# An adaLN attention and GLU block: eight query blocks of 256 instead of four of 512, with side work between the scores

## The chip, the cores and the metric

The kernel runs on one core of one Trainium2 chip. The metric is device time in microseconds. The core has five engines that run at the same time: TensorE (PE; its weight loads are listed apart as PEld), VectorE (DVE), ScalarE (ACT), GpSimd (POOL) and SyncE (SP), which here only issues transfers. Each engine works through its own instructions in the order in which the program was written; between engines only semaphores make one wait for another.

## The reference

The computation is a transformer block on 2048 tokens of width 512: a conditioned layer norm, multi-query attention with 32 heads of width 16 that share one key and one value, and a gated product of two projections.

```python
mod = (_silu(c) @ w_mod).reshape(1, 6, 1, -1)          # six rows of 512
h = _layernorm(x) * (1 + ca) + sa
q = (h @ wq) split into 32 heads of 16;  k = h @ wk;  v = h @ wv
scores = einsum("bhqd,bkd->bhqk", q, k) * 16 ** -0.5
o = softmax(scores) @ v
x = x + ga * (o @ wo)
h = _layernorm(x) * (1 + cb) + sb
x = x + gb * (((h @ w_gate) * (h @ w_up)) @ w_down)    # inner width 1792
```

Inputs and output are 32-bit floats. The kernel scales the large operands and splits each into two 16-bit halves, so that a product becomes three 16-bit products that are added up.

## The kernel before, in words

**Units and steps.** The 2048 queries are taken in four blocks (`NB`) of 512 (`BT`). A unit is four heads of a block, so a block has eight units (`UB`) and there are 32 (`NU`). A unit has 32 steps. In each step TensorE writes two tiles of scores with queries on partitions (`max_mm`, written to banks named mx), whose row maxima VectorE takes (L565); two tiles of scores with keys on partitions, the maxima already subtracted (`qk_exp`, banks sc), whose exponentials ScalarE takes (L601, tile P); and one product of earlier exponentials with the values (`pv`, 32-bit, L609). Maxima run 38 steps (`LEAD`) ahead of the exponentials: the first 38 steps have maxima alone and share their time with the first norm and the projections of keys, values and the first queries. Once a unit's maxima are complete they are transposed and split (`max_rows`, L577 to L583) and sent by two transfers into the stationary tile sst (L586), as two more rows of the score product.

**Row halves.** All these products use 64 of the array's 128 rows and 32 of its columns at a time: four matmuls (`quarters`, L474) make one row half of a tile. Work on the upper and the lower row half can be in the array at the same time, if they write to different banks.

**Side work.** Everything else on TensorE in the loop goes through a list (`fill`): the query projections (`q_proj`, tiles h and wq), the output projection (`wo_work`, och and wo), the gate and up products (h2T with wg and wu) and the down product (glu with wd). A `duo` takes two output tiles at once, one on each row half, and swaps them half way; a pair is one matmul group on each row half, eight matmuls. At the end of each step `fill_gap` writes a burst of up to three pairs, at a rate that `pace` works out from the due times of all that is listed. The work that belongs to a block begins one unit after the block's last.

**Rows after attention.** `pv_out` adds two partial sums on VectorE (L621), sends heads to a tile oc and the softmax sums to memory (L628, L629); `normalise` fetches them (L636), inverts (L639), spreads them (L641, L643), multiplies and splits on POOL (L648 to L651). `wo_work` ends with the second norm's statistics (L697 to L715), and four single items transpose the normed rows (L740) into h2T (L747 to L750). Those four items run alone: no pair is written until they are through.

**Late weights.** Three weight matrices and wo are read twice in slices into tiles wsl (L870). The first time POOL squares them and adds them up (L877, L879), ones on TensorE sum over partitions (L889) and VectorE takes the maxima of these sums (L892); that gives scales. The second time POOL scales and splits them (L966 to L974). `side_step` writes one such item every 2.5 steps.

**The tail.** After the last unit the last block's rows still need their output projection, norm, gate, up and down products. They run as plain matmuls on all 128 rows and columns (`plain`, L521). What is left in `fill` by then (`RESERVE`) covers the waits of the last normalisation and norm.

Of the kernel before, what the change touches and what calls it, by code (L numbers as in the profile page):

```python
# [13 lines left out]
F32 = mybir.dt.float32  # L14
# [7 lines left out]
NB = 4  # L22
BT = S // NB
UB = H // 4
NU = NB * UB
# [3 lines left out]
ABS_GAP = 2.5  # L29
SPLIT_GAP = 2.5  # L30
NSC = 2
NMX = 2
NP = 5
CW = 32
# [5 lines left out]
RESERVE = 31000.0  # L40
TR_GAP = 8
# [4 lines left out]
Q_BURSTS = {16: 4, 17: 2, 18: 2, 19: 2, 20: 2, 22: 6, 23: 6}  # L46
DUE = 12
QDUE = 236
# [5 lines left out]
def adaln_mqa_glu_kernel(ctx: ExitStack, tc: tile.TileContext, x_in, wq_in, wk_in, wv_in, wo_in,  # L54
# [48 lines left out]
    wqs = work.tile([128, KC, 64], F32, name="wqs", tag="xl", bufs=3)  # L103
    nc.scalar.dma_start(wqs, wq_in[:, 0:64].rearrange("(k p) n -> p k n", p=128))
# [8 lines left out]
    wk3 = work.tile([128, KC, 2, 64], F32, name="wk3", tag="och", bufs=4)  # L113
    nc.gpsimd.memset(wk3, 0.0)
    wq0 = [work.tile([128, KC, 2, 64], F32, name="wq0", tag="och", bufs=4) for _ in range(2)]
    for w in wq0:
        nc.gpsimd.memset(w, 0.0)
    wqst = [work.tile([128, D], F32, name="wqst", tag=("gf", "oc")[k // 2], bufs=2) for k in range(KC)]
# [83 lines left out]
    h16 = big.tile([128, 2, KC, S], F16, name="h16", tag="big")  # L202
# [85 lines left out]
    for h in range(4):  # L288
        nc.gpsimd.tensor_copy(wq0[h // 2][:, :, h % 2, 0:48].rearrange("p k (r e) -> p k r e", e=16),
                              wqs[:, :, None, 16 * h:16 * h + 16].to_broadcast([128, KC, 3, 16]))  # L290
# [4 lines left out]
    mrow = work.tile([128, 256], F32, name="modrow", tag="xl", bufs=3)  # L295
# [39 lines left out]
    def q0_mm(p, ks=range(KC)):  # L335
        if 0 in ks:
            pqs[p] = ps_misc() if p else ps_pv()
        for k in ks:
            nc.tensor.matmul(pqs[p], wq0[p][:, k].rearrange("p a r -> p (a r)"), hf(0, k),
                             start=(k == 0), stop=(k == KC - 1))  # L340
# [62 lines left out]
    def h_halves(b, ks=range(KC)):  # L403
        cs = slice(b * BT, (b + 1) * BT)
        for k in ks:
            in_halves(h16[:, 0, k, cs], h16[:, 1, k, cs], hf(b, k),
                      None if b else fwd[:, 0:1], nc.scalar if b > 1 else nc.gpsimd)
# [18 lines left out]
    first = {0: lambda: q0_mm(1, KA), 1: lambda: (q0_mm(1, KB), ln_stats(6)),  # L426
# [15 lines left out]
    def v_mm(k):  # L442
# [3 lines left out]
        for i, (wl, hl) in enumerate(TERMS):  # L446
            for b in range(NB):
                nc.tensor.matmul(p[32 * b:32 * b + 32, :], wv[:, wl, k, :], h16[:, hl, k, b * BT:(b + 1) * BT],
# [18 lines left out]
    class Group:  # L467


        def __init__(self, n, op, pre, post, mid=True):  # L470
            self.n, self.op, self.pre, self.post, self.mid = n, op, pre, post, mid

    def quarters(p, left, right, start=True, stop=True):
        return [nc.tensor.matmul(p[c:c + CW, :], left[:, c:c + CW], right, start=start, stop=stop)  # L474
                for c in range(0, 128, CW)]

    def half(p, g, i, r, start, stop):
        left, right = g.op(i)
        return quarters(p, left[64 * r:64 * r + 64], right[64 * r:64 * r + 64], start, stop)
# [4 lines left out]
    def duo(g0, g1, tags=("misc", "spare")):  # L484

        ps = g0.pre(tag=tags[0]), g1.pre(tag=tags[1])
        n = g0.n
        mark = None
        for turn in range(2):
            for i in range(n):  # L490
                for r in range(2):
                    ms = half(ps[r ^ turn], (g0, g1)[r ^ turn], i, r, turn == 0 and i == 0,
                              turn == 1 and i == n - 1)
                    if mark is not None:
                        tc.add_manual_dep(ms[0].ins, mark.ins.name, SYNC, reason="row halves of one bank in turn")
                        mark = None
                if turn == 0 and i == n - 1 and cur["mark"]:
# [779 lines left out]
```

## Time and profile before

| | |
|---|---|
| median of 3 runs | 1772.2 us (1771.98 to 1772.65) |
| the profiled execution | 1771.55 us, span 1769.7 us |
| granted TensorE clock | 0.994 of full speed |
| busy share PE / DVE / ACT / POOL | 96 / 81 / 74 / 32% |
| maxima on VectorE (L565) | 2048 of 685 ns |
| exponentials on ScalarE (L601) | 2048 of 601 ns |
| plain matmuls (L521) | 720, 379 ns each with the pipeline's own delay |

Rows of the profile's groups read: line, engine, operation, tile written, tiles read, shape, count, then the busy time of the group in us and the mean of one in ns, then the idle time of the engine before them and what ended it. Matmuls overlap, so a sum of their means is far more than the busy time. Windows give, for each stretch, its length and the busy time and count of each engine in it, then the clock, the share of the DMA engines and GB/s.

### The profile page before, as it was taken

The page shows a single profiled execution, that of the slowest core. Times are in us where ns is not written, and L with a number is a line of the kernel's source. Part 1 is how long each engine was busy: PE and PEld are TensorE (multiplying, and loading weights), DVE is VectorE, ACT ScalarE, POOL GpSimd, SP SyncE. Part 2 cuts the span into 40 slices and gives each one's busy share as a digit, 9 for nine tenths or more (in the row PEclk, how much of TensorE's full clock was granted, in tenths as well). Part 3 has the DMA queues.
Part 4 walks back from the last instruction along what each step waited for, and adds up shares of the span by engine and source line. Part 5 has one row for each costly group of instructions (what it writes and reads, how often), then busy time and mean ns, then how long its engine had stood idle before and what let it go on. Part 6 is the DMA issues. An engine that isn't in the chain of part 4 may idle for free. (4 is left out here: it accounts for less than half of the span.)

```text
span 1769.7 us, 86400 instructions
## 1 busy us (share of the span) xinstructions
PE 1707.4 (96%) x39203; PEld 878.6 (50%) x39203; DVE 1442.1 (81%) x2353; ACT 1301.8 (74%) x2319; POOL 562.5 (32%) x788
## 2 busy tenths in 40 slices
PE   6899999999999999999999999999999999999999
PEld 3334444433345565565545555565545555543444
DVE  7899999999998888899998888899999998922210
ACT  3478888878878878887788888887888888893110
POOL 5714444436657852210032222110032121221130
PEclk9999999999999999999999999999999999999999
DMA  5212222212222210000100000000100000001000
GB/s 195 100 32 80 60 80 62 77 46 73 80 74 58 66 34 15 11 19 23 42 23 18 11 10 20 7 16 24 48 16 18 12 18 11 14 7 41 19 0 24
DMA packets 49115, 70.04 MB, mean 40 GB/s; under 512 B 15270, under 2 KB 29418, under 8 KB 48748
## 3 DMA queue, kind: packets, MB, share of 16 engines
q1 hardware_dynamic: 47164, 64.33, 12.2%
q8 instruction: 306, 5.01, 1.2%
q14 instruction: 61, 0.50, 0.1%
q10 hardware_dynamic: 1584, 0.20, 0.1%
HBM read 51.12 MB, written 8.92 MB: 34 GB/s over the span
## 5 line engine op out<-in xcount | busy, mean ns | idle before, releaser
L565 DVE TENSOR_REDUCE mpart<-mx 128x1 f32<-128x512 f32 x2048 | 1329.0, 685 | 125.9 <-PE mx L474 36.1
L601 ACT ACTIVATE P<-sc 128x512 f32<-128x512 f32 x2048 | 1177.0, 601 | 259.9 <-PE sc L474 203.7
L609 PE MATMUL pv<-P,vst 64*32 64x512 f32 x8192 | 1080.8, 598 | 0.0
L474 PE MATMUL mx<-kst,sst 48*32 48x512 f16 x8192 | 808.4, 383 | 35.7 <-DVE mpart L565 27.2
L474 PE MATMUL sc<-sst,kst 50*32 50x512 f16 x8192 | 818.5, 379 | 5.3 <-ACT P L601 4.5
L474 PEld LDWEIGHTS <-sst 48*32 48x32 f16 x8192 | 335.6, 90 | 514.4 <-issue 420.9
L474 PEld LDWEIGHTS <-kst 50*32 50x32 f16 x8192 | 264.2, 92 | 92.7 <-issue 60.7
L474 PE MATMUL misc<-h2T,wu 64*32 64x512 f16 x4032 | 294.8, 376 | 0.0
L474 PE MATMUL misc<-h2T,wg 64*32 64x512 f16 x4032 | 294.2, 376 | 0.0
L609 PEld LDWEIGHTS pv<-P,vst 64*32 64x32 f32 x8192 | 197.8, 105 | 17.9 <-ACT P L601 0.8
L791 POOL TENSOR_TENSOR gf<-gf,g 128x512 f32<-128x512 f32 x42 | 53.7, 1279 | 344.2 <-ACT gf L790 344.2
L474 PEld LDWEIGHTS <-wu 64*32 64x32 f16 x4032 | 111.0, 92 | 36.1
L474 PEld LDWEIGHTS <-wg 64*32 64x32 f16 x4032 | 112.9, 92 | 30.7 <-issue 1.5
L474 PE MATMUL misc<-wd,glu 64*32 64x512 f16 x2688 | 112.9, 376 | 0.0
L474 PE MATMUL misc<-h,wq 64*32 64x512 f16 x1536 | 95.4, 377 | 1.2 <-ACT qf L531 1.2
L498 POOL MEMSET token<- 1x1 f32 x43 | 3.8, 88 | 281.4 <-PE misc L474 216.7
L783 ACT ACTIVATE g<-misc 128x512 f32<-128x512 f32 x56 | 33.4, 596 | 77.0 <-PE misc L521 75.5
L521 PE MATMUL misc<-wd,glu 128*128 128x512 f16 x336 | 73.2, 379 | 0.0
L474 PEld LDWEIGHTS <-glu 64*32 64x32 f16 x2688 | 60.3, 92 | 23.4 <-issue 0.4
L795 POOL TENSOR_TENSOR glu<-gf,glu 128x512 f16<-128x512 f32 x56 | 65.0, 1161 | 4.7
L793 DVE TENSOR_TENSOR gf<-misc,g 128x512 f32<-128x512 f32 x14 | 9.7, 692 | 62.9 <-PE misc L521 62.9
L621 DVE SCALAR_TENSOR_TENSOR ev<-pv,evs,ev 128x512 f32<-128x512 f32 x32 | 23.7, 742 | 44.5 <-ACT ev L616 44.5
(232 smaller groups left out, 1063.1 us busy)
## 6 DMA issues: line engine op xcount, KB each, us to landing
wsl<-in_B_w_gate_dram SPq DMA_DIRECT2D x32, 224.0 KB
wsl<-in_B_w_up_dram SPq DMA_DIRECT2D x32, 224.0 KB
wsl<-in_B_w_down_dram SPq DMA_DIRECT2D x28, 256.0 KB
sst<-qd SPq DMA_DIRECT2D x186, 32.0 KB
qd<-q SPq DMA_DIRECT2D x16, 256.0 KB
oc<-ev SPq DMA_DIRECT2D x128, 32.0 KB
rr<-ri SPq DMA_DIRECT2D x16, 256.0 KB
xl<-in_A_x_dram SPq DMA_DIRECT2D x16, 256.0 KB
```

Source lines behind the costliest of these rows:

```text
L474: return [nc.tensor.matmul(p[c:c + CW, :], left[:, c:c + CW], right, start=start, stop=stop) for c in range(0, 128, CW)]
L498: mark = nc.gpsimd.memset(token, 0.0)
L521: nc.tensor.matmul(p, left, right, start=i == 0, stop=i == g.n - 1)
L565: nc.vector.tensor_reduce(mparts[u][:, a, p, t, kc:kc + 1], m, axis=AX.X, op=OP.max)
L601: nc.scalar.activation(ptl[u, kt, a][:, p, :], t, AF.Exp)
L609: nc.tensor.matmul(pvb[u, r][32 * j:32 * j + 32, :], vst[ks, kt, :], ptl[u, kt, a][ks, p, :], start=(kt == 0), stop=(kt == KT - 1))
L621: nc.vector.scalar_tensor_tensor(ev, pvb[u, 1], evs, ev, op0=OP.mult, op1=OP.add)
L783: nc.scalar.activation(st["g", f], p, AF.Copy, scale=2.0 ** -45)
L791: nc.gpsimd.tensor_tensor(gf, gf, st["g", f], op=OP.mult)
L793: nc.vector.tensor_tensor(gf, p, st["g", f], op=OP.mult)
L795: nc.gpsimd.tensor_tensor(st["glu"][:, 1, f, :], gf, st["glu"][:, 0, f, :], op=OP.subtract)
```

## The change

- The queries are taken in eight blocks (`NQ`) of 256 (`QT`). A unit is now eight heads of such a block, two of them side by side in the 512 columns of a tile, so there are still 32 units of 32 steps with the same score, maximum, exponential and value instructions; a block has four units. `load_q` needs twelve transfers for it instead of six, `pv_out` nine instead of five, and each unit is normalised alone, on half as many columns.
- Gate and up products have 256 tokens and so 256 columns. A group holds two such products side by side in one bank (`parts=2`): sixteen matmuls of half the length to a pair. Down and output products keep their 512 columns and have two tiles of rows to a block.
- A pair may be cut: in a step with side work, its first row half is written between the first exponential's scores with the value product and the second maximum, the other row half after the second scores, and the rest of the burst behind it (`pair_half`).
- The transposes of the second norm leave `fill` and go, two to a block, into the banks of the maxima, at fixed steps after the output projection. The down product of a block waits until after the next block's output projection.
- Row maxima are issued one step later than they are ready, from ScalarE's queue.
- ScalarE squares the late weights, and for wo and the down weights a sum over all takes the place of column sums; items come every 1.5 steps in the first pass and every 2.0 in the second. Products start when the slices they need have been written (`ready`).
- The input of the query projection lies in two tiles, the projections are due at step 140 instead of 236, twice as many run in the first 38 steps, and `RESERVE` falls from 31000 to 20000.

```diff
-UB = H // 4
-NU = NB * UB
+NQ = 8
+QT = S // NQ
+UB = H // 8
+NU = NQ * UB
...
-RESERVE = 31000.0
+RESERVE = 20000.0
...
+    def product(p, g, i, j, rows, start, stop):
+        left, right = g.op(i) if g.parts == 1 else g.op(i, j)
+        w = 512 // g.parts
+        start, stop = start and j == 0, stop and j == g.parts - 1
+        p, left, right = p[:, j * w:(j + 1) * w], left[rows], right[rows]
+        if rows.stop - rows.start == 64:
+            return quarters(p, left, right, start, stop, skip_group_check=g.parts > 1)
+        nc.tensor.matmul(p, left, right, start=start, stop=stop, skip_group_check=g.parts > 1)
...
-            for hl in range(2):
-                nc.sync.dma_start(s[48 + hl:113 + hl:64, :, :], mt[hl])
+
+            def send():
+                for hl in range(2):
+                    nc.scalar.dma_start(s[48 + hl:113 + hl:64, :, :], mt[hl])
+
+            after(1, send)
...
+            if m > 1:
+                nc.scalar.activation(t, t, AF.Square, accum_out=fro[:, m - 2, i:i + 1])
+                return
             acc = ssq[:, c]
-            nc.gpsimd.tensor_tensor(acc if i == 0 else t, t, t, op=OP.mult)
+            nc.scalar.activation(acc if i == 0 else t, t, AF.Square)
...
+    def pair_half(step, r):
+        what = cur["gen"].emit(r)
+        if cur["gen"].done:
+            return
+        credit[0] -= 1.0
+        cur["left"] -= 1
+        cur["turn"] -= 1
...
+            n = 0
+            if fill or cur["gen"]:
+                credit[0] = min(credit[0] + pace(step) / 2, 6.0)
+                n = plan(step)
             max_half(a, 0, 2)
             qk_exp(u, kt, 0, a)
...
             drain_mids()
+            if n:
+                pair_half(step, a)
             max_half(a, 1, 2)
             qk_exp(u, kt, 1, a)
+            if n:
+                pair_half(step, 1 - a)
+                burst(step, n - 1)
             if p == 1:
                 late_max()
-            if fill or cur["gen"]:
-                credit[0] = min(credit[0] + pace(step) / 2, 6.0)
-                if credit[0] >= 1.0:
-                    fill_gap(step)
...
-        gu = [(Group(3 * KC, op(f, 0), pre(f), gate(f)), Group(3 * KC, op(f, 1), ps_misc, up(f))) for f in range(FT)]
-        return gu, [Group(3 * FT, dn(t), ps_misc, fin(t)) for t in range(4)]
+        gu = [(Group(3 * KC, op(f, 0), pre(f), gate(f), parts=2), Group(3 * KC, op(f, 1), ps_misc, up(f), parts=2))
+              for f in range(FT // 2)]
+        return gu, [Group(3 * FT, dn(t), ps_misc, fin(t)) for t in range(2)]
```

How the instructions move, at three places. TensorE in a step amid the gate and up products: mx are the maxima's scores, sc the exponentials', pv the value product, wg and wu the two tiles of a pair. Before, a burst stands behind the second sc; one matmul of each group is shown.

```order
L474 MATMUL mx<-kst,sst_122 32x512
...
L474 MATMUL sc<-sst_120,kst 32x512
...
L609 MATMUL pv<-P,vst 32x512 x4
...
L474 MATMUL mx<-kst,sst_122 32x512
...
L474 MATMUL sc<-sst_120,kst 32x512
...
L474 MATMUL misc<-h2T,wg 32x512
...
L474 MATMUL misc<-h2T,wu 32x512
```

The same in the change:

```order
L485 MATMUL mx<-kst,sst_124 32x512
...
L485 MATMUL sc<-sst_123,kst 32x512
...
L641 MATMUL pv<-P,vst 32x512 x4
...
L485 MATMUL misc<-h2T,wg 32x256
...
L485 MATMUL mx<-kst,sst_124 32x512
...
L485 MATMUL sc<-sst_123,kst 32x512
...
L485 MATMUL misc<-h2T,wu 32x256
```

One row half of a pair has moved between the two maxima, and its four matmuls of 512 columns have become eight of 256.

ScalarE in the first unit: P are exponentials, mt the split row maxima, wsl a slice of weights, fro its sum of squares. Before:

```order
L601 ACTIVATE P<-sc 128x512 x56
L582 ACTIVATE mt_2250<-mxt 16x128
L601 ACTIVATE P<-sc 128x512 x12
L616 ACTIVATE ev<-pv,evs 128x512
L601 ACTIVATE P<-sc 128x512 x32
```

In the change:

```order
L633 ACTIVATE P<-sc 128x512 x4
L923 ACTIVATE wsl,fro<-wsl 128x512
L633 ACTIVATE P<-sc 128x512 x4
L926 ACTIVATE kwb<-wsl 128x448
...
L926 ACTIVATE wsl<-wsl 128x448
L616 DMA sst_124<-mt_2436 2x8x128
L616 DMA sst_124<-mt_2437 2x8x128
```

A square now stands behind every fourth exponential, and the two transfers of the row maxima, which were SP's, stand among the exponentials.

TensorE in the tail, at the first gate and up products of the last block: before and in the change.

```order
L521 LDWEIGHTS wg
L521 MATMUL misc<-h2T,wg 128x512
...
L521 LDWEIGHTS wu
L521 MATMUL misc<-h2T,wu 128x512
```

```order
L495 LDWEIGHTS wg
L495 MATMUL misc<-h2T,wg 128x256
...
L495 LDWEIGHTS wu
L495 MATMUL misc<-h2T,wu 128x256
```

The last block is half as long: 336 matmuls of 512 columns for its gate and up products have become 336 of 256, and it has two tiles of rows for each of the other products instead of four.

More of the change, by code (lines that the diff above doesn't have):

```diff
@@ L481, in adaln_mqa_glu_kernel @@
     token = consts.tile([1, 1], F32, name="token")
     SYNC = mybir.DependencyInfo(mybir.DependencyClass.Sync, mybir.DependencyReason.DATA)
[L484 to L497, printed above, removed]
-                    mark = nc.gpsimd.memset(token, 0.0)
-                    tc.add_manual_dep(mark.ins, ms[-1].ins.name, SYNC, reason="end of a row half")
-                if turn == 0 or i < n - 1:
-                    yield i == n - 1
-        g0.post(ps[0])
-        def late():
-            g1.post(ps[1])
-            after(3, free)
-        def free():
-            spare["held"] -= 1
-        spare["held"] += 1
-        if g1.mid:
-            mids.append(late)
-        else:
-            after(2, late)
@@ new lines, in adaln_mqa_glu_kernel, with __init__, emit, late @@
+    class Duo:
+        def __init__(self, two, tags, marked):
+            self.g = two
+            self.ps = [g.pre(tag=tag) for g, tag in zip(two, tags)]
+            self.n, self.turn, self.i, self.done, self.marked, self.mark = two[0].n, 0, 0, set(), marked, None
+        def emit(self, r):
+            w = r ^ self.turn
+            g, n = self.g[w], self.n
+            for j in range(g.parts):
+                ms = product(self.ps[w], g, self.i, j, slice(64 * r, 64 * r + 64),
+                             self.turn == 0 and self.i == 0, self.turn == 1 and self.i == n - 1)
+                if self.mark is not None:
+                    tc.add_manual_dep(ms[0].ins, self.mark.ins.name, SYNC, reason="row halves of one bank in turn")
+                    self.mark = None
+            self.done.add(r)
+            if len(self.done) < 2:
+                return None
+            self.done.clear()
+            self.i += 1
+            if self.i < n:
+                return None
+            if self.turn == 0:
+                self.turn, self.i = 1, 0
+                if self.marked:
+                    self.mark = nc.gpsimd.memset(token, 0.0)
+                    tc.add_manual_dep(self.mark.ins, ms[-1].ins.name, SYNC, reason="end of a row half")
+                return "swap"
+            self.g[0].post(self.ps[0])
+            spare["held"] += 1
+            if self.g[1].mid:
+                mids.append(self.late)
+            else:
+                after(2, self.late)
+            return "end"
+        def late(self):
+            self.g[1].post(self.ps[1])
+            after(3, self.free)
+        def free(self):
+            spare["held"] -= 1
@@ L519, in plain @@
         for i in range(g.n):
-            left, right = g.op(i)
-            nc.tensor.matmul(p, left, right, start=i == 0, stop=i == g.n - 1)
+            for j in range(g.parts):
+                product(p, g, i, j, slice(0, 128), i == 0, i == g.n - 1)
             if i < g.n - 1:
@@ L846, in m1 @@
         def m1():
-            st["row"] = work.tile([128, D], F32, name="modrow", tag="xl", bufs=3)
+            st["row"] = work.tile([128, D], F32, name="modrow", tag="xl", bufs=NXL)
             nc.scalar.activation(st["row"], st["p"], AF.Copy)
@@ L926, in bc @@
             nc.tensor.matmul(st["p"][:, 0:6], ones6, st["r"][:, 1:7], start=True, stop=True)
+            nc.tensor.matmul(st["p"][:, 8:10], ones, cmx[:, 2:4], start=True, stop=True)
         def scales():
@@ L1066, in open_gate @@
         gate = fill[0][0]
+        if len(gate) > 2 and ready[0] < gate[2]:
+            return False
+        if len(gate) > 3 and step < ln_end.get(gate[3], END) + LN_WAIT:
+            return False
         if gate[0] is None:
@@ L1222, in adaln_mqa_glu_kernel @@
         assert cur["second"] and NU * NSTEP - cur["swapped"] > 2
-        for _ in cur["gen"]:
+        while cur["gen"] is not None:
             drain_posts()
+            burst(NU * NSTEP, 1)
+        drain_posts()
         drain_mids()
```

337 lines of the change are left out of this document (179 added, 158 removed).

## The prediction

> **What bounds the kernel now.** I read the engines' busy shares on the page first, then windows cut at the loop's units, then the waits, the chain that ended last and single stretches of the timeline. All times are in the profiled execution: span 1769.7 us, its own time 1771.55 us, so 1.85 us lie around the span; the median of the runs, 1772.2 us, is 0.04% above it.
>
> The windows below begin and end with a unit's first and last exponential. Columns: stretch and length, then busy us and count for PE, PEld, DVE, ACT, POOL.
>
> ```profile
> PE 1707.4 (96%) x39203; PEld 878.6 (50%) x39203; DVE 1442.1 (81%) x2353; ACT 1301.8 (74%) x2319; POOL 562.5 (32%) x788
> ...
> 93.70:273.40 179.70, 174.44 (x3796) 73.39 (x3796) 168.54 (x278) 153.43 (x269) 69.66 (x71) 0.98 0.21 60
> 229.90:273.40 43.50, 42.54 (x969) 18.38 (x961) 41.42 (x68) 38.71 (x68) 22.05 (x24) 1.00 0.29 81
> 503.00:553.70 50.70, 47.96 (x1137) 25.61 (x1128) 45.70 (x75) 41.85 (x76) 37.84 (x68) 0.97 0.26 70
> 652.20:701.50 49.30, 48.90 (x1409) 30.14 (x1401) 43.37 (x69) 39.70 (x73) 13.86 (x17) 1.00 0.07 17
> 1567.50:1605.80 38.30, 36.46 (x739) 13.29 (x727) 0.75 (x1) 36.30 (x69) 6.20 (x7) 1.00 0.03 7
> 93.70:1605.80 1512.10, 1476.04 (x37717) 777.30 (x37720) 1339.25 (x2151) 1249.61 (x2232) 470.95 (x614) 1.00 0.13 35
> 1605.80:1769.70 163.90, 158.62 (x750) 72.17 (x746) 29.22 (x47) 15.30 (x23) 32.52 (x60) 1.00 0.07 22
> ```
>
> The loop of 32 units is 1512.1 us; behind it stands a tail of 163.9 us in which only TensorE works (158.62 busy). The same windows for the tiles called misc give the side work of a unit; eight matmuls are one pair of row halves:
>
> ```profile
> 229.90:273.40 43.50, 13.19 (x192) 0.00 (x0) 0.00 (x0) 1.39 (x2) 1.00 0.29 81
> 503.00:553.70 50.70, 16.95 (x352) 1.68 (x16) 1.49 (x2) 3.79 (x5) 0.97 0.26 70
> 652.20:701.50 49.30, 25.82 (x624) 0.00 (x0) 0.00 (x0) 3.61 (x6) 1.00 0.07 17
> 1380.60:1428.10 47.50, 22.57 (x488) 0.00 (x0) 0.00 (x0) 3.60 (x6) 1.00 0.05 11
> 1428.10:1474.60 46.50, 22.66 (x480) 0.00 (x0) 0.00 (x0) 2.42 (x4) 1.00 0.07 18
> 1522.20:1567.50 45.30, 22.86 (x484) 0.00 (x0) 0.00 (x0) 2.42 (x4) 1.00 0.05 14
> 1567.50:1605.80 38.30, 10.13 (x216) 0.00 (x0) 0.00 (x0) 2.42 (x4) 1.00 0.03 7
> 93.70:1605.80 1512.10, 613.90 (x13296) 5.05 (x48) 14.83 (x20) 70.24 (x110) 1.00 0.13 35
> ```
>
> A unit with 24 pairs takes 43.5 us, with 60.5 (mean of two) 47.0, with 78 it is 49.3. So a pair costs (47.0 − 43.5)/36.5 = 0.096 us up to 60 and 2.3/17.5 = 0.13 beyond: less than its own time on the array (0.216, below), since the array also waits. In the full units neither VectorE (43.37 of 49.3) nor ScalarE is full; the three engines wait on each other in turn. The whole loop holds (13296 − 48 transposes)/8 = 1656 pairs.
>
> **The tail** is the surest term.
>
> ```profile
> 1641.05 124.77 PE misc L521 x578
> ```
> ```profile
> 1605.80:1769.70 163.90, 156.09 (x720) 70.28 (x720) 1.00 0.07 22
> ```
>
> One plain matmul of 512 columns comes every 124.77/578 = 0.216 us, and 720 of them fill the tail. In the change's order the tail keeps 192 of 512 columns (168 down, 24 output projection) and 384 of 256. A short one costs between half (0.108) and, if the weight load behind it sets the pace, all of 0.216; I take 0.109, by the half, since the row above shows 70.28/720 = 0.098 us of weight load for each, just less. New: 192 × 0.216 + 384 × 0.109 = 83.4; old: 155.5. With 1 us more of idle time, as the cover work is thinner, the tail falls by 71 us (bounds 30 and 72).
>
> **The loop gets what the tail loses.** By the order it now holds 1968 pairs: none in the first unit, then 42.5, 41.5, 43.5, 37 and 31, about 55 in each of the next three, 69.2 in each of the next twenty, then 81, 84 and 59.5. By the two slopes: 37 and 31 pairs, 44.7 + 44.2 = 89; three at 46.5 = 139.4; twenty at 47.0 + 8.7 × 0.13 = 48.1 = 962; 81 pairs 49.7; the next to last 45.3 + 23 × 0.13 = 48.3; the last, where ScalarE is 95% busy and hides pairs, 39.5. The first four are ScalarE's: it now squares the 50 weight slices that POOL squared.
>
> ```profile
> L601 ACT ACTIVATE P<-sc 128x512 f32<-128x512 f32 x2048 | 1177.0, 601 | 259.9 <-PE sc L474 203.7 <-ACT P L601 1.3
> L377 ACT ACTIVATE wqj<-wqst 128x512 f32<-128x512 f32 x4 | 2.5, 628 | 0.1
> L377 ACT ACTIVATION_READ_ACCUMULATOR wqj<-wqst 128x1 f32 x4 | 0.7, 186 | 0.0
> L531 ACT ACTIVATE qf<-misc,qvs 128x512 f32<-128x512 f32 x16 | 11.1, 691 | 4.3 <-PE mx L474 2.3 <-POOL q L533 2.0
> ...
> 1567.50:1605.80 38.30, 34.30 (x64) 1.00 0.03 7
> ```
>
> Where ScalarE alone sets the pace, 64 exponentials are 34.3 us. Four units: 137.2; 32 squares of 448 columns at 0.628 × 448/512 = 0.55, 17.6; 18 with a sum at 0.81, 14.7; 10 projections at 0.69 and some 3 us of small ones, 9.9; in all 179.4, and at the 95% that the last unit reaches 189 us. Before, 179.7. Sum of the loop: 189 + 89 + 139.4 + 962 + 49.7 + 48.3 + 39.5 = 1517.
>
> Added to it: the second norm. The unit at 503 us, which holds it, takes 50.7 with (352 − 16)/8 = 42 pairs, 5.5 above the slope, for four tiles of rows; seven blocks of two tiles, 2.75 each, 19 us (from 0, if that excess was the pause in the side work alone, to 38). And POOL, which splits the weights faster than before:
>
> ```profile
> L972 POOL TENSOR_SCALAR wsl<-wsl,sca 128x448 f32<-128x448 f32 x32 | 20.4, 639 | 22.6 <-DMA wsl<-in_B_w_gate_dram 12.4 <-DMA wsl<-in_B_w_up_dram 10.1
> L973 POOL TENSOR_SCALAR wu<-wsl 128x448 f16<-128x448 f32 x16 | 9.0, 565 | 1.3
> L974 POOL TENSOR_TENSOR wu<-wsl,wu 128x448 f16<-128x448 f32 x16 | 16.6, 1040 | 1.3
> ```
>
> 2.24 us a slice, 17 slices in the sixth unit are 38 us of a unit of 44, beside the halves of the norm and of the first gate, so POOL falls behind there. Late POOL keeps load buffers, SP's later transfers stand behind those loads, and the row sums that VectorE inverts come late. I take 5 us (0 to 10). The loop is then 1541, 29 above before. That 312 more pairs cost so little has a reason: laid over the units of before the two slopes give 1478 of the 1512, and the other 34 are extras that shrink or move (16 the norms, most of the rest the weights' column sums of the first eight units, which the change cuts from 16 to 4).
>
> **Side halves between the scores.** One half now stands between the two row maxima of a step. Does TensorE use it?
>
> ```profile
> 1011.95 0.40 PE L474 MATMUL misc<-h2T,wg 64*32 64x512 f16 x4
> 1012.00 0.60 PE L609 MATMUL pv<-P,vst 64*32 64x512 f32 x4
> 1012.16 0.40 PE L474 MATMUL mx<-kst,sst 48*32 48x512 f16 x4
> 1012.38 0.40 PE L474 MATMUL sc<-sst,kst 50*32 50x512 f16 x4
> ```
>
> In the program mx and sc stand ahead of pv, yet pv, on the other row half, starts first: each half runs on by itself, so a half placed earlier can fill idle time. The most it can bring is a full unit at the pace of the lightest, 48.1 − 43.5 = 4.6 us in each of 20 units, 92 us; the least is nothing. Of some 4.3 halves a step one is moved between the maxima, so I take a quarter, 23 us. The Trainium skill (TensorE: Matmul & The Clock Gate, Part 3, "What overlaps and what doesn't") says that matmuls keep program order in start and end. By that rule the moved half gains nothing and the time would be 23 us more; the pv at 1012.00 ahead of the mx at 1012.16 disagrees.
>
> **The rest.** The head takes 24 more projection pairs, 24 × 0.216 = 5.2 us, bounds 0 and 10. Row maxima from ScalarE's queue:
>
> ```profile
> SPq L586 <- ACT mt L582: 472.1, 27, 38.0
> ...
> PE mx L474 <- DVE mpart L565: 27.2, 73, 1.2
> ...
> PE sc L474 <- ACT P L601: 4.5, 14, 1.1
> ...
> 903.07 0.55 SPq L629 DMA_DIRECT2D rs<-ev  x1
> ```
>
> SP spends 472 us on waiting to send them, but TensorE's scores wait for no transfer, so the move wins nothing. Two issues of 0.55 us a unit now stand among the exponentials: 1.1 us, hidden while ScalarE has 9 us a unit to spare; without that cover 4.4 us in the first four units, inside the 189. SP's own issues (21 small transfers a unit for queries and outputs instead of 11) are 21 × 0.55 = 12 us of 48, on an engine with nothing else to do.
>
> **The sum:** 1769.7 − 71 + 5.2 + 29 − 23 = 1709.9 span, and 1.85 around it: **1712 us**, 3.4% faster.
>
> **Rivals.**
>
> *The short matmuls cannot be fed.* A gate/up pair was 16 instructions on TensorE and is now 32; by the order 1152 of the loop's pairs are such. The densest ten microseconds of a full unit:
>
> ```profile
> 713.80:723.80 10.00, 10.00 (x324) 6.63 (x324) 8.65 (x13) 7.85 (x14) 2.65 (x4) 1.00 0.02 5
> ```
>
> That is 30.9 ns a matmul. A unit with 69 gate/up pairs has 768 + 69 × 16 = 1872 matmuls, 25.7 ns each at 48.1 us; at 30.9 it takes 57.8. Of four units two are dense (+9.7 and +6.8), one mixed (+2), one with down products alone unharmed: 18.6 × 5 = 93, with the early and last units 125 us: 1837, slower. It decides from about 29 ns a matmul. For it: nothing here shows a denser stretch. Against it: the array itself set that pace (10.00 busy), and a burst goes faster:
>
> ```profile
> 60.57 1.06 PE L474 MATMUL misc<-h,wq 64*32 64x512 f16 x32
> 60.57 0.56 PEld L474 LDWEIGHTS <-wq 64*32 64x32 f16 x32 [0.17 <-issue]
> ...
> L474 PE MATMUL misc<-h2T,wg 64*32 64x512 f16 x4032 | 294.2, 376 | 0.0
> ```
>
> 32 weight loads began within 0.5 us. The same page ("Wait — 56ns, not 53.3ns?") puts a floor of about 25 ns between starts, however short the matmul; by it 16 would take 0.40 us, and 1152 such pairs 207 us more if nothing hid it. Four starts of a group lie within 0.40 − 0.376 us in the rows above, so it does not hold across column strips.
>
> *The halves do more.* All of the 92 us: 1643. For it: full units leave 12% of VectorE idle. Against: three quarters of the side work stay in bursts.
>
> *The halves do nothing:* 1735. VectorE's two banks could still set the pace.
>
> *The loop takes all back.* At a full 0.216 for each of 312 added pairs, 67 us instead of the 30 by the slopes, and no help from the halves, the loop is 1541 + 37 = 1578 and the time 1769.7 − 71 + 5.2 + 66 + 1.85 = 1772: no change. For it: TensorE is busy 48.90 of 49.3 in a full unit. Against it: the slopes are measured, and half of that.
>
> **How the numbers follow.** Two measurements can be told apart from about 0.2%, 3.5 us. Forecast 0.48, 1680 to 1730; halves do more 0.16 (1640 to 1680); halves do nothing 0.18 (1730 to 1760). Together 0.82 faster. Not fed 0.10; all taken back 0.08, of which 0.05 within 0.2% of before and 0.03 above: same 0.05, slower 0.13. The range for 8 in 10, 1645 to 1772, leaves out the slow cases and the lower end of the halves.
>
> **What would show it.** Right: a tail of about 92 us with 576 plain matmuls, units of 47 to 48 us at 69 pairs, the first four at 47 each with ScalarE over 90% busy. Wrong: gate/up units longer than down units at equal pairs (feeding); full units of 44 us (halves do more); waits of a score for a transfer or of the weights for POOL between 350 and 450 us. If the short plain matmuls come at more than 0.12 us, the tail was mis-sized.

## The result and the profile after

The changed kernel takes 1898.75 us (median of four runs, 1897.56 to 1902.64) against 1772.09 for the kernel before: 1.072 times as long, 95% interval 1.0701 to 1.0738. The forecast was 1712. The tail did what was forecast; the loop did not.

Windows of the changed kernel, with the columns of the prediction's (stretch and length; busy us and count for PE, PEld, DVE, ACT, POOL; clock, DMA share, GB/s). First a unit that holds down products and a block's second norm, then one of gate/up behind the last nine down pairs, one of gate/up alone, the loop and the tail:

```profile
787.40:836.50 49.10, 48.10 (x1369) 29.77 (x1364) 43.66 (x72) 41.52 (x73) 9.36 (x24) 1.00 0.06 14
836.50:892.70 56.20, 50.49 (x1807) 34.91 (x1788) 44.91 (x71) 39.89 (x71) 8.16 (x12) 1.00 0.08 23
892.70:951.00 58.30, 54.42 (x1886) 35.10 (x1891) 43.35 (x69) 40.58 (x72) 11.13 (x14) 1.00 0.05 13
101.80:1805.00 1703.20, 1587.79 (x49334) 972.52 (x49321) 1358.31 (x2165) 1303.69 (x2328) 437.86 (x644) 0.99 0.12 32
1805.00:1895.20 90.20, 85.66 (x598) 57.26 (x594) 15.21 (x26) 9.62 (x16) 19.33 (x33) 1.00 0.07 22
```

The tail is 90.2 us (163.9 before). The loop is 1703.2 (1512.1 before, 1518 forecast), and the head grew from 93.7 to 101.8. The same windows for the tiles called misc:

```profile
787.40:836.50 49.10, 35.01 (x580) 0.00 (x0) 0.00 (x0) 0.00 (x0) 1.00 0.06 14
836.50:892.70 56.20, 35.77 (x1032) 0.00 (x0) 1.48 (x2) 2.42 (x4) 1.00 0.08 23
892.70:951.00 58.30, 35.94 (x1112) 0.00 (x0) 0.00 (x0) 3.60 (x6) 1.00 0.05 13
```

A down pair is eight matmuls and a gate/up pair 16, so the first unit holds 72.5 pairs in 49.1 us and the third 69.5 in 58.3. Fewer pairs take longer, and PE is idle for 3.9 us in a unit in which no other engine is near full. The waits of PE say for what (columns: engine, line, what ended the wait, us in total, times, longest):

```profile
PE misc L485 <- issue: 37.7, 80, 1.2
PE sc L485 <- ACT P L633: 29.7, 33, 5.4
...
PE mx L485 <- issue: 6.7, 11, 1.3
PE pv L641 <- issue: 4.4, 9, 0.7
PE sc L485 <- issue: 4.3, 11, 1.1
```

Four of the rows end in "issue": PE waited for nothing that the profile shows, for 53 us in 111 pauses. The same view of the kernel before has no such row. The second row is another loss, of single stalls up to 5.4 us in the early units. I take them in turn.

**The pauses come every 256 instructions.** Three of them, from the timeline of PE (start, length, then the idle time before in brackets):

```profile
853.88 0.29 PE L485 MATMUL misc<-h2T,wg 64*32 64x256 f16 x4 [0.52 <-issue]
...
857.90 0.29 PE L485 MATMUL misc<-h2T,wg 64*32 64x256 f16 x4 [0.73 <-issue]
...
861.92 0.29 PE L485 MATMUL misc<-h2T,wg 64*32 64x256 f16 x4 [0.73 <-issue]
```

Windows cut from one pause's end to the next:

```profile
853.88:857.90 4.02, 3.28 (x128) 2.68 (x128) 2.93 (x6) 2.52 (x5) 0.00 (x0) 1.00 0.05 6
857.90:861.92 4.02, 3.29 (x128) 2.67 (x128) 2.67 (x4) 2.39 (x4) 0.00 (x0) 1.00 0.16 45
```

Each holds 128 matmuls and 128 weight loads and lasts 4.02 us. Over the whole run, 59 of the 110 distances from one pause to the next are 248 to 264 instructions (matmuls and weight loads together), and 16 more are twice that. Two DMA queues on the page move instructions, and one of them, q8, has PE's count (packets, MB, share of the DMA engines); the changed kernel, then the kernel before:

```profile
q8 instruction: 398, 6.52, 1.5%
```
```profile
q8 instruction: 306, 5.01, 1.2%
```

These are 398 packets for 2 x 50885 instructions of PE and 306 for 2 x 39203: 256 instructions, a block, in each. The count fits to within one packet in all 16 profiles of this case. Of the 111 pauses, 101 end 0.8 to 1.6 us before a packet of this queue starts, against one moment in five by chance. That is the order one would see if entering a block of 256 sends for the next one, and PE stands still where it has used its block up before the next is there; the store itself is not in the profile. A gate/up unit of 1886 matmuls needs 2 x 1886/256 = 14.7 blocks, and 58.3/14.7 = 3.96 us each.

**The early units.** ScalarE, SP, PE and VectorE around the stall at 216 us:

```profile
207.01 5.65 SPq L660 DMA_DIRECT2D oc<-ev  x8
212.76 0.53 SPq L916 DMA_DIRECT2D wsl<-in_B_w_up_dram  x1
...
215.69 0.58 ACT L926 ACTIVATE wsl<-wsl 128x448 f32<-128x448 f32 x1 [5.18 <-DMA wsl<-in_B_w_up_dram]
...
216.81 0.61 PE L485 MATMUL sc<-sst,kst 50*32 50x512 f16 x4 [5.21 <-ACT P L633]
...
218.89 0.69 DVE L593 TENSOR_REDUCE mpart<-mx 128x1 f32<-128x512 f32 x1 [6.54 <-PE sc L485]
```

SP issues a unit's eight output transfers for 5.65 us; the load of a weight slice stands behind them; ScalarE, in its order, waits 5.18 us at that slice's square; the exponentials wait behind it, then the scores, then VectorE. Afterwards the clock is lower for a while: the score took 0.61 us, where one takes 0.40 at full clock, and over the unit the granted clock was 0.94:

```profile
199.00:257.00 58.00, 50.05 (x1121) 24.10 (x1113) 43.02 (x71) 45.50 (x92) 18.15 (x20) 0.94 0.30 90
```

Units 1 to 5 took 54.0, 57.8, 57.8, 52.1 and 57.1 us. The longest stall of PE, 5.4 us at 340 us in unit 4, has another source:

```profile
339.27 0.69 ACT L558 ACTIVATE qf<-misc,qvs 128x512 f32<-128x512 f32 x1 [5.07 <-POOL q L560]
```

Here ScalarE waits in its order for POOL's part of an earlier query projection, and in POOL's order that part stands behind splits of weight slices.

### The profile page after: what moved, and what is told of

Read it like the earlier page. It is cut to its first block, busy times and chain, and to the rows that moved or that the text cites. A ratio compares the mean times of both kernels' runs of the same rounds, so it can differ in the third digit from the quotient of the medians.

```text
span 1895.2 us, 110249 instructions
## 1 busy us (share of the span) xinstructions
PE 1750.8 (92%) x50885; PEld 1064.7 (56%) x50885; DVE 1448.6 (76%) x2348; ACT 1351.5 (71%) x2410; POOL 520.8 (27%) x801
## 4 chain that ended last, share of the span: by engine, by line
PE 75%; DVE 7%; issue 6%; ACT 5%; POOL 3%; DMA 2%; SPq 1%; ACTq 0%; DVEq 0%; POOLq 0%
PE misc L485 24%; PE pv L641 18%; PE mx L485 15%; PE sc L485 13%; DVE mpart L593 5%; PE misc L495 4%; ACT P L633 3%; SPq L660 1%; ACT hf L786 1%; POOL h L410 1%; DMA wsl<-in_B_w_gate_dram 1%; DMA wsl<-in_B_w_up_dram 0%; PE mx L777 0%; DVE x L728 0%; SPq L580 0%
## 5 line engine op out<-in xcount | busy, mean ns | idle before, releaser
L641 PE MATMUL pv<-P,vst 64*32 64x512 f32 x8192 | 1119.1, 605 | 4.4 <-issue 4.4
L485 PE MATMUL sc<-sst,kst 50*32 50x512 f16 x8192 | 846.5, 382 | 38.6 <-ACT P L633 29.7
L485 PEld LDWEIGHTS <-sst 48*32 48x32 f16 x8192 | 303.5, 91 | 328.6 <-issue 236.4
L485 PE MATMUL misc<-h2T,wu 64*32 64x256 f16 x9216 | 424.0, 270 | 17.0 <-issue 16.4
L485 PE MATMUL misc<-h2T,wg 64*32 64x256 f16 x9216 | 419.3, 270 | 21.5 <-issue 21.3
L485 PEld LDWEIGHTS <-wg 64*32 64x32 f16 x9216 | 244.6, 91 | 94.2 <-issue 43.9
L485 PEld LDWEIGHTS <-wu 64*32 64x32 f16 x9216 | 239.6, 91 | 94.9 <-issue 45.5
L485 PE MATMUL misc<-wd,glu 64*32 64x512 f16 x4032 | 244.1, 376 | 0.0
L485 PEld LDWEIGHTS <-glu 64*32 64x32 f16 x4032 | 99.0, 92 | 36.3 <-issue 1.8
L485 PE MATMUL misc<-wo,och 64*32 64x512 f16 x1344 | 79.4, 376 | 0.0
```

The costliest lines, as they stand in the source:

```text
L641: nc.tensor.matmul(pvb[u, r][32 * j:32 * j + 32, :], vst[ks, kt, :], ptl[u, kt, a][ks, p, :], start=(kt == 0), stop=(kt == KT - 1))
```

## The experiments

### Is it the count of instructions? One part alone, on the kernel before

```diff
-        return quarters(p, left[rows], right[rows], start, stop)
+        if g.short:                       # gate and up
+            for j in range(2):
+                c = slice(256 * j, 256 * j + 256)
+                ms += quarters(p[:, c], left[rows], right[rows, c], ...)
```

> The kernel before, with one edit: a gate or up half streams its 512 queries as two matmuls of 256, so a pair is 32 instructions instead of 16, with the same columns streamed and the same order of everything else. Feeding theory: its gate/up units of 78 pairs go from 1409 to some 2030 matmuls with as many weight loads, 15.9 packets of 256 instructions at 3.7 to 4.0 us, 59 to 64 us instead of 49.3; units with down products alone keep their 47; over the loop 1008 such pairs, the time goes from 1772 to 1900 to 1970. Rival (what counts is the columns streamed, and the length of the changed kernel's gate/up units comes from its order): 1772 to 1785.

Measured: 1878.92 us, 1.0608 (1.0551 to 1.0664), below the 1900 to 1970 expected: units with some 60 gate/up pairs grew by only 3 to 6 us, those with 78 by about 10. Windows of this run: a unit of gate/up, one of down products, the loop:

```profile
670.90:730.10 59.20, 52.09 (x2021) 35.56 (x2002) 44.39 (x69) 39.66 (x72) 13.77 (x17) 1.00 0.06 15
834.60:883.30 48.70, 47.69 (x1389) 29.33 (x1381) 44.32 (x70) 37.30 (x67) 0.09 (x1) 1.00 0.08 22
92.50:1707.20 1614.70, 1530.78 (x45774) 870.50 (x45771) 1352.10 (x2151) 1246.71 (x2232) 470.29 (x614) 1.00 0.12 33
```

The same down unit in the kernel before:

```profile
798.00:846.70 48.70, 47.69 (x1388) 29.30 (x1387) 44.28 (x70) 37.31 (x66) 0.09 (x1) 1.00 0.08 22
```

The gate/up unit takes 59.2 us for what took 49.3; the down unit keeps its 48.7. Nothing of the order was touched and no column added. The count of matmuls, with a weight load for each, is enough to make a unit long.

The same edit with four matmuls of 128 columns in place of two of 256:

```diff
-            for j in range(2):
-                c = slice(256 * j, 256 * j + 256)
+            for j in range(4):
+                c = slice(128 * j, 128 * j + 128)
```

> The kernel before with a gate or up half streamed in four matmuls of 128 queries: 64 instructions a pair, against 32 in the run with two of 256 and 16 before; the columns streamed are the same. Against the run with two of 256 (1879 us, 369 instruction packets) it has 126 more packets of 256 instructions, nearly all in units that the packets already set. Feeding theory: each costs its whole interval of 3.4 to 4.0 us, together 428 to 504 us, 2305 to 2385. If 1879 came from something that 256 columns have and is not a matter of the count (weight loads no longer hidden behind short matmuls, say), the rise is of the size of the first step, 105 us, some 1985, or with the weight load of 0.1 us for each group of four, beyond what 128 columns take (0.054), some 0.05 x 8064 / 2 = 200 us, 2080.

One run: 2342.14 us, within the 2305 to 2385 of the feeding theory, and far from the 1985 and 2080 of weight loads that are no longer hidden. It has 495 packets of q8 against 369 in the run above; these 126 more cost 463 us, 3.7 us each. Window of the same unit, and the waits:

```profile
752.60:850.30 97.70, 71.26 (x3281) 48.13 (x3269) 45.32 (x69) 40.39 (x72) 13.46 (x16) 0.90 0.05 11
```
```profile
PE misc L474 <- issue: 278.0, 223, 2.0
```

(3281 + 3269)/256 = 25.6 blocks in 97.7 us, 3.8 us each. The granted clock was 0.90 in this unit; what share of the 463 us that made stays open.

### The changed kernel without the extra instructions

```diff
-    for j in range(g.parts): ... quarters(p[:, j * w:(j + 1) * w], left_j[rows], right[rows], ...)
+    right = right[rows][:, None, :].to_broadcast([64, 2, QT])     # the 256 queries twice
+    quarters(p, left_0[rows], right, ...)
```

> The changed kernel, but a gate or up half in the loop is one set of four matmuls of 512 columns that reads the block's 256 queries twice; the second chunk of 128 hidden columns is left out and the first stands in its place. Columns streamed, tile shape (64 by 32), banks, evictions and order stay; a pair is 16 instructions instead of 32. Feeding theory (256 instructions need about 4.0 us): the pauses without a releaser vanish, gate/up units at 69 pairs fall from 55.7 to 58.3 us to 48 to 50, the cycle of four from 215 to about 195, the time from 1899 to 1755 to 1790. Rival (the halves between the scores, or the norm's transposes in the banks of the maxima, make these units long): they stay at 55 us or more, time above 1880.

In the loop this kernel leaves out half of the hidden columns' products and computes the other half twice. Measured: 1772.91 us, 126 less than the changed kernel, 0.9996 (0.9986 to 1.0006) of the kernel before. A cycle of four units, and the loop:

```profile
661.70:709.50 47.80, 47.35 (x1329) 27.32 (x1329) 43.17 (x69) 40.75 (x73) 11.14 (x14) 1.00 0.06 14
709.50:758.20 48.70, 47.53 (x1313) 27.31 (x1308) 44.98 (x73) 39.89 (x72) 8.20 (x12) 1.00 0.09 25
758.20:807.20 49.00, 48.00 (x1367) 29.70 (x1362) 43.53 (x71) 41.45 (x72) 9.34 (x24) 1.00 0.05 14
807.20:855.70 48.50, 47.00 (x1329) 27.31 (x1321) 44.23 (x71) 39.97 (x70) 8.17 (x12) 1.00 0.09 25
99.40:1676.80 1577.40, 1511.87 (x40119) 844.98 (x40105) 1348.97 (x2165) 1304.02 (x2328) 437.58 (x644) 0.99 0.12 34
```

A cycle takes 194 us instead of 213 to 217, and no wait of PE ends in "issue" any more. The placement of halves and the norm's transposes are in this kernel too, so they do not make the units long. The edit takes away matmuls and weight loads alike; that it is their number, and not the time of the loads, rests on the pauses at 256 and on the run with 128 columns. The price of the instruction supply in the changed kernel is 126 us. The 53 us of pauses are the part of it that shows as idle time of PE; where the rest lies stays open.

### Fewer instructions by wider tiles

```diff
-    quarters(p, left, right, start, stop, skip_group_check=...)            # four of 32 columns
+    quarters(p, left, right, start, stop, w=CW * g.parts, ...)             # gate/up: two of 64
```

> The changed kernel, but a gate or up half is two matmuls of 64 stationary columns instead of four of 32: a pair of 256 queries is again 16 instructions, half of the 32 it has in the changed kernel, at the same columns streamed. Feeding theory (TensorE gets its instructions in packets of 256, and a packet cannot follow the one before in less than about 4.0 us): the pauses without a releaser go, gate/up units at 69 pairs fall from 55.7 to 58.3 us to 48 to 50, a cycle of four units from 215 to about 195, and the time from 1899 to 1760 to 1800. Placement rival (the halves between the scores, or the transposes in the banks of the maxima, make the gate/up units long): these stay at 55 us or more, the time at 1880 to 1900. Third possibility (changing between tiles of 64 and 32 columns drains the array): slower than 1899.

> The changed kernel with 64 stationary columns for every half-row product (scores, maxima, projections, gate, up, down), so that only the weighted sums keep 32: a unit's TensorE instructions fall by about 60% of their number against the changed kernel's 1807 to 1886 matmuls. Feeding theory: no pause without a releaser is left, units of 69 pairs at 48 us or less, time 1730 to 1790, no slower than the kernel in which gate and up alone are wide. If changing the tile width drains the array, this one is clearly faster than that one, since only the weighted sums still change it. Placement rival: 1880 to 1900 again. If 64 columns run less well side by side than 32, scores get longer than 0.40 us and units longer than before.

(The second sets CW = 64 for all of them.) Measured: 2289.7 us, 1.287 (1.2776 to 1.297), and 4079.8 us, 2.30 (2.296 to 2.3029). The first has the instruction count of the run above, and PE's timeline shows where the time goes:

```profile
1060.99 0.61 PE L641 MATMUL pv<-P,vst 64*32 64x512 f32 x4
1061.53 0.41 PE L485 MATMUL misc<-h2T,wg 64*64 64x256 f16 x4
1061.87 0.40 PE L485 MATMUL mx<-kst,sst 48*32 48x512 f16 x4
1062.09 0.39 PE L485 MATMUL sc<-sst,kst 50*32 50x512 f16 x4
1062.41 0.30 PE L485 MATMUL misc<-h2T,wu 64*64 64x256 f16 x2
```

In this stretch no product of one width runs beside one of the other: the wide half begins as the weighted sum ends, and the next maximum waits for the wide half. A unit of gate/up and one of down products (32 columns throughout) in the same run:

```profile
1071.90:1150.20 78.30, 78.05 (x1325) 27.10 (x1321) 45.00 (x69) 41.09 (x73) 11.07 (x14) 1.00 0.03 8
948.80:997.80 49.00, 48.01 (x1369) 29.63 (x1361) 43.57 (x71) 41.44 (x73) 9.34 (x24) 1.00 0.05 14
```

So the third possibility held. The Trainium skill says it too (TensorEngine Tiling (Array Packing), "Key Properties": changing the tiling mode drains TensorE), and this trace agrees. Because of it this pair says nothing on the supply. The second run did not come out faster than the first, as was expected of a mere drain: its clock fell and stayed down, though PE was busy all the time, so it does not test the drain (the clock row of its page in 40 slices, and a window):

```profile
PEclk9555555555555555555555555555555555555559
```
```profile
2000.00:2050.00 50.00, 50.00 (x436) 17.65 (x432) 18.52 (x28) 16.11 (x28) 4.92 (x7) 0.50 0.08 21
```

### The early stalls: the squares' engine, or the loads' distance

```diff
-            nc.scalar.activation(acc if i == 0 else t, t, AF.Square)
+            nc.gpsimd.tensor_tensor(acc if i == 0 else t, t, t, op=OP.mult)
```

> The changed kernel, but the 32 squares of gate and up slices are computed on POOL again; the 18 with a sum stay on ScalarE. Theory (in units 1 to 3 ScalarE, in order, waits in a square for a weight slice whose load stands on SP's queue behind eight output transfers, and the exponentials behind it stop the scores): the stalls of 3.6 to 5.4 us of TensorE near 160, 217 and 272 us go, units 1 to 3 fall from 53.9, 57.8 and 57.8 us to 45 to 50, the loop and the time by 20 to 35 us, to 1864 to 1879. Rival (the side work of these units itself is long, or the slower clock in them has another cause): less than 8 us gained. POOL gets 32 times 0.8 us more to do, and if it is what these units wait for, they get longer.

Measured: 1894.59 us, 1.0679 (1.0663 to 1.0695), 4 us less; the loop is 1700.0 instead of 1703.2. Units 1 and 2 fell to 51.5 and 51.9, unit 3 kept 57.9. The stalls at 160 and 217 us went and others came, as this row of PE's timeline, a column sum behind POOL's additions:

```profile
164.59 0.56 PE L938 MATMUL mx<-kwb,onec 128*32 128x224 f32 x2 [1.53 <-POOL kwb L928]
```

The theory's price, 20 to 35 us, was wrong; moving the waiting instruction moved the wait.

```diff
-LAG = 2
+LAG = 3
```

> The changed kernel with a weight slice loaded three work items ahead of its square or its split, not two (4.5 steps instead of 3, about 6.5 us instead of 4.5). Theory (a load stands behind eight output transfers, 5.65 us, on SP's queue, so the square that ScalarE meets in order is late): the stalls of TensorE near 160, 217 and 272 us, 12.6 us together, go, and with them the half-speed clock behind each (3.4, 6.8 and 10.2 us, half of it lost, 10 us): units 1 to 3 fall from 54.0, 57.8 and 57.8 us to about 50, the time by 15 to 25 us, to 1874 to 1884. Rival (as with the squares on POOL, where one stall went and another came: the next late thing is POOL's halves of a projection or its column sums): 0 to 8 us.

Measured: 1875.60 us, 1.0579 (1.0558 to 1.06), 23 less, within the theory's 15 to 25. The stall at 216 us in this run:

```profile
203.40 5.62 SPq L660 DMA_DIRECT2D oc<-ev  x8
209.11 0.53 SPq L916 DMA_DIRECT2D wsl<-in_B_w_up_dram  x1
...
212.61 0.58 ACT L926 ACTIVATE wsl<-wsl 128x448 f32<-128x448 f32 x1 [2.83 <-DMA wsl<-in_B_w_up_dram]
```

The transfers still stand ahead, but the wait is 2.83 us instead of 5.18, and those at 160 and 272 us are gone; units 1 to 3 took 49.4, 54.7 and 52.6, together 13 us less, and units 4 and 5 another 5. So the loads' lateness behind SP's transfers is what stalled PE at these three places, and one item more is not quite enough.

The 512-column halves and LAG = 3 in one kernel:

> The changed kernel with both edits: gate and up halves as one set of four matmuls of 512 columns that reads the 256 queries twice (the second chunk of hidden columns is left out), and weight slices loaded three work items ahead. Alone they gave 126 and 23 us. If the two causes are separate, 1899 - 126 - 23 = 1750 (1745 to 1756). If the early stalls were part of the same shortage, the second edit adds under 10 us: 1763 or more.

Both edits together: 1753.18 us, 0.9888 (0.9874 to 0.9902), 146 less than the changed kernel; 149 was the sum. These are two separate causes.

### What is left: the squares and the sends

From that run, once with the sends of the row maxima on SP's queue again and without the delay of one step, once with 42 of the 50 squares left out:

```diff
-            after(1, send)                       # nc.scalar.dma_start(s[...], mt[hl])
+            for hl in range(2): nc.sync.dma_start(s[48 + hl:113 + hl:64, :, :], mt[hl])
```

> The run with gate and up halves of 512 columns and loads three items ahead (1753 us; the second chunk of hidden columns is left out), with the row maxima sent from SP's queue again, at once and not one step later. On the kernel before, the move to ScalarE's queue had cost 13 us, 0.4 us in nearly every unit. If the price is that of two issues among the exponentials, it is the same here: 1753 - 13 = 1740 (1737 to 1743). If units that hold more side work hide it: 1750 to 1753. If the sends on SP now stand behind the 21 small transfers of a unit and a score waits for them: slower than 1753.

```diff
-            if m > 1: nc.scalar.activation(..., AF.Square, accum_out=...); return
+            if m > 1 or i: return
```

> The run with gate and up halves of 512 columns and loads three items ahead (1753 us; the second chunk of hidden columns is left out), with 42 of the 50 squares of weight slices left out as well, so that ScalarE neither computes them nor waits for their loads; the loads and the splits stay. If the squares hold units 1 to 3 (49.3, 54.1 and 52.9 us), these fall to 45 to 47, the price of 41 to 44 pairs by the slopes, and the time by 12 to 20 us, to 1733 to 1741. If what is left there is POOL's halves of the projections behind its other work, units 1 to 3 stay above 49 and units 4 and 5 at 50.6 and 51.4: 1745 to 1753.

Measured: 1740.86 us, 0.9812 (0.9796 to 0.9829), and 1736.19 us, 0.9789 (0.9775 to 0.9804). The sends, with their delay, cost 12 us. In the profiled executions 6.5 of that lie in the loop (1557.4 against 1550.9) and 4.2 in the head, 104.4 against 100.2; but in the other runs of the changed kernel, with the sends on ScalarE's queue, the head took 99.4 to 102.9, so the 4.2 are not shown to be theirs. The second edit also leaves out POOL's 24 additions of squares and every wait for these loads. All of that cost 17 us: units 1 to 3 fell from 49.3, 54.1 and 52.9 to 47.3, 48.0 and 49.2, some 2 us above the theory's 45 to 47, and units 4 and 5 stayed at 49.9 and 51.8.

### The halves and the sends, each alone

```diff
-            if n: pair_half(step, a)
             max_half(a, 1, 2)
             qk_exp(u, kt, 1, a)
+            if n: pair_half(step, a)
             if n: pair_half(step, 1 - a); burst(step, n - 1)
```

> The changed kernel with both halves of a side pair behind the second score of the step, as before the change, and nothing else different. The prediction's term (a half between the scores fills idle time of TensorE, 23 us over the loop): 23 us slower, 1922. If the supply of instructions sets the pace of the gate/up units, their number is the same and the order hardly matters there: within 8 us of 1899, with what difference there is in the units without gate/up pairs (48.5 to 49.0 us now). Rival (a half in front of the second row maximum delays VectorE): 10 to 40 us faster.

Measured: 1896.35 us, 1.0695 (1.0671 to 1.0719), not to be told from the changed kernel. In the kernel with the short instructions the order makes no difference that can be told. A unit of down products takes 50.0 instead of 49.1:

```profile
785.80:835.80 50.00, 49.39 (x1362) 30.73 (x1361) 43.53 (x72) 40.91 (x72) 9.33 (x24) 1.00 0.05 13
```

The reverse move, the kernel before with a half between its scores:

```diff
             drain_mids()
+            if n: first_half()
             max_half(a, 1, 2)
             qk_exp(u, kt, 1, a)
-            fill_gap(step)                       # n pairs, both halves
+            if n: burst(step, n, begun=True)     # second half, then n - 1 pairs
```

> The kernel before, with the one part of the change alone that puts the first half of a side pair between the two scores of a step. At 1409 matmuls a unit of 49.3 us the supply of instructions does not bind it (11 packets of 256 at 4.0 us are 44 us), so the placement shows by itself. Prediction's term, scaled from 1968 to 1656 pairs: 19 us faster, 1753. Nothing gained: 1768 to 1776. Delay of the second score and its exponential: slower, 1780 or more.

Measured: 1761.15 us, 0.9931 (0.9912 to 0.995), 12.5 us faster than before. This is a version that beats both kernels.

On top of it, the sends from ScalarE's queue one step later, or RESERVE = 20000.0:

> The kernel before with the first half of a side pair between the scores (1761 us) and the row maxima sent from ScalarE's queue one step later. Prediction's step: the sends win nothing and cost nothing, since no score waits for one: 1761, within 4. If two issues of 0.55 us among the exponentials are not hidden, 32 x 1.1 = 35 us are the most: 1765 to 1796. If SP, freed of 472 us of waiting, starts its other transfers earlier and something waited for them: faster than 1757.

> The kernel before with the first half between the scores, and the tail's reserve cut from 31000 to 20000 (the value of the change): some 50 pairs move from the tail, where one takes 0.216 us, into the last eight units. By the slope of the units, 0.096 to 0.13 us a pair, the loop grows by 5 to 6.5 us and the tail falls by 10.8: 1755 to 1757 instead of 1761. If the last units are full and a pair costs there what it costs in the tail: 1761. Of the tail's work enough is left (93 pairs, 20 us) to cover the last normalisation.

With the sends on ScalarE's queue: 1773.90 us, 1.0008 (0.9999 to 1.0017). They take the whole gain back, 12.7 us, with the loop 11.6 longer. The timeline of ScalarE and its queue shows the place:

```profile
700.57 0.60 ACT L607 ACTIVATE P<-sc 128x512 f32<-128x512 f32 x1
700.63 1.13 ACTq L590 DMA_DIRECT2D sst<-mt  x2
701.81 1.69 ACT L607 ACTIVATE P<-sc 128x512 f32<-128x512 f32 x3 [0.64 <-PE sc L474]
```

The next exponential starts only when both issues, 1.13 us, are through. The bracket puts the wait down to a score, but in 31 of the 32 units ScalarE's next instruction starts 0.05 us after the second issue, with 0.6 us or more of idle time before it. That is 20 us in all, of which 11.6 show in the loop. The smaller reserve gives 1759.03 us, 0.9924 (0.9911 to 0.9937): between the two expected, and not to be told from 1761. It moved 84 pairs, not the 50 expected (636 plain matmuls are left of 720). The loop grew by 8.7 us, 0.10 a pair, as the slopes have it; the tail fell by 10.4, not by 84 x 0.216 = 18.

## Why the prediction was wrong

The step that failed first of all is the price of a gate/up pair in the loop; some smaller terms failed beside it.

- **The tail: right.** 90.2 us, about 92 forecast; the short plain matmuls cost what their columns cost (384 in 44.6 us, 0.116 each, 0.109 forecast). The head grew by 8.1 us, within its bounds (5.2, 0 to 10).
- **The second norm, 19 us: not to be seen.** The first unit above holds it and 72.5 pairs in 49.1 us; the slopes alone give 47.0 + 12 x 0.13 = 48.6. That leaves 0.5 a block where 2.75 were added.
- **The price of a pair by the slopes: right for the array, wrong for the supply.** Without the extra instructions the cycle of four is 194 us; the slopes gave 4 x 48.1 = 192.4. What failed is that the slopes, taken from pairs of 16 instructions, were used for pairs of 32: the sum had nothing for the doubled count. Measured for it: 126 us.
- **The rival "the short matmuls cannot be fed" was what happened.** It was given its point of decision (29 ns a matmul; measured 3.7 to 4.0 us for 128 matmuls with their loads, 29 to 31 ns) and its price (125 us; measured 126), and a chance of 0.10. What spoke against it was misread. The densest 10 us of the kernel before hold 324 matmuls and as many loads, 2 x 324/256 = 2.53 blocks, 3.95 us each: that stretch already ran at the pace of the limit, and that PE was busy for all 10.00 us could not show which of the two set it. And 32 loads begun within 0.5 us can be a burst out of a block that is already there; they say nothing of a rate that holds over 256. The Trainium skill describes such a supply (Runtime: NRT & Kernel Launch, "Instruction fetch mechanics"): instructions come in blocks of 256, by a queue of the engine's own. This trace agrees on the block (398 packets for 101770 instructions). The Trainium skill calls the cost mostly hidden; here it was 53 us of pauses and 126 in all.
- **The first four units, 47 us each by ScalarE's load: wrong in three of them.** They took 43.3, 54.0, 57.8 and 57.8, 24 more than the 189. ScalarE was busy for 93% of the first but for only 76 to 81% of the others, where over 90% had been forecast: it waited, and its load did not set the pace. Loads three items ahead took 13 us out of units 1 to 3, and leaving out 42 squares with their waits another 12. With loads in time the four units still took 199 us; only without those squares, which the forecast had included, did they take 188. The prediction counted SP's added transfers (12 us of 48, "on an engine with nothing else to do") and did not ask which load stands behind them.
- **POOL, 5 us: too small.** Units 4 and 5 took 109 us where 89 and POOL's 5 were forecast, and 102 with both repairs (halves of 512 columns, loads three items ahead). In that run PE still stalls for 4.3 us at 328 us, at the place where ScalarE waits for POOL; the rest is open.
- **The sends from ScalarE's queue, at nothing: wrong.** They cost 12 and 13 us in the two pairs of runs, 6.5 and 11.6 of it in the loop, with the delay of one step in both. "ScalarE has 9 us a unit to spare" was an average; the exponential right behind the issue was on the path. And one score did wait for a transfer: the first of the changed kernel's loop, for 1.6 us.
- **The halves between the scores, 23 us: the right sign, on the kernel before** (12.5 for 1656 pairs, 19 by the prediction's scale). The size was a share by count, with no row for it, and half as much again as what came. In the changed kernel nothing could be told.
- **The sum.** 1899 - 1712 = 187: 146 for the supply and the late loads together. With both repairs the profiled span is 1752.3 us, still 42 above the forecast's 1709.9: 6 in the head, 10 in units 0 to 3, 8 in units 4 and 5, 22 in the rest of the loop, and 2 less in the tail. The sends are 6.5 us in the loop. What else lies in the 22 stays open; the forecast had taken 23 off the loop for the halves.

The range, 1645 to 1772, missed, and "faster" had 0.82.

## What to carry to other kernels

Count instructions per unit of time as a resource of its own, matmuls and weight loads together, and compare with the densest stretch of a few hundred instructions, not with a burst; where a change halves the length of matmuls, that number doubles and the columns do not tell it. When transfers are added to a queue, list what stands behind them and who meets it in order. A spare share of an engine does not hide work that is issued right ahead of the instruction others wait for.

## What the runs showed of the hardware

TensorE's instructions arrive in packets of 256 (398 packets for 101770 in the changed kernel). Where they were the limit, one packet took 3.7 to 4.0 us, 14.5 to 15.7 ns an instruction. Two issues of transfers on ScalarE's queue took 1.13 us, and its next instruction started 0.05 us after them. Products of 64 x 32 and 64 x 64 tiles did not overlap in the stretch shown of the run that mixed them. The clock came back to full after ordinary stalls (0.91 to 0.97 in units 1 to 5 of the changed kernel, 1.00 in unit 6), but in the run with 64 columns throughout it stayed at half in 38 of 40 slices of the span, some 3870 us, with PE busy all the time. Why it did is open.
